# A shorter lag of the second matmuls, a later preparation in block 0, and a rearranged boot and end in a fused RWKV-6 and tanh-shrink kernel

## The chip, the cores and the metric

The kernel runs on one core of a Trainium2 chip. The metric is the device time of one execution in microseconds (us). Below, PE is TensorE, DVE is VectorE, ACT is ScalarE, POOL is GpSimd and SP is SyncE, as the profile has them.

## The reference

The first part is a recurrence over time steps in each of 4 batches and 8 heads, with a state of 48 x 48. The second part is a dense layer of 384 to 2048 to 384 over the 3072 tokens, with `h - tanh(h)` between its two matrix products.

```python
# r, k, v, w: (4, 8, 768, 48), u: (8, 48), all float32
for t in range(S):
    cur = np.einsum('bhd,bhe->bhde', u[None] * kt, vt)
    y[:, :, t] = np.einsum('bhd,bhde->bhe', rt, state + cur)
    state = wt[:, :, :, None] * state + np.einsum('bhd,bhe->bhde', kt, vt)
x = y.transpose(0, 2, 1, 3).reshape(3072, 384)
h = x @ w_in                    # (384, 2048)
out = (h - np.tanh(h)) @ w_out  # (2048, 384)
```

## The kernel before

The tokens are cut into 8 blocks of 384: two blocks (`q`) in each of four batches. A block's recurrence is computed in chunks of 64 tokens: masked products of keys and receptances inside a chunk (`own`, `earlier`), a state per chunk (`update_1` on PE, `update_2` on DVE), and results from states and from scores (`result`). The eight heads are four pairs, and the pairs are two halves, named 2 and 0 by their first pair. The block's preparation on DVE consists of running products of the decays: `behind` (line 300) with `inverse` (321, 323), `before` (289), and their products with keys and receptances, `times_behind` (314) and `times_before` (307). On ACT there are `times_u` (328) and `bound` (334).

The dense part of a block runs in 16 steps `f`. In a step, `first` (line 626) makes three matmuls with `w_in` into one PSUM tile `hp`, which ACT copies to `h`; `slight` (638) computes `s = h*h` with its largest value on DVE; `Second.add` (671) multiplies `g` with `w_out` into three accumulators. Every float32 matmul is two instructions in the profile. The operations after `s` (`qa` on ACT, `hs` and `gT` on DVE) are kept in `rest` and come behind the next step's `s`. The second matmuls of step f are put behind those of `first` of step f + LAG, through the list `waiting`; LAG is 4 before the change, also across the border of two blocks.

All queues (PE, DVE, ACT and SP) run in the order in which the program is written. While block i goes through its dense steps, block i + 1 (`later`) is prepared and its recurrence computed, at the steps that `plan` (685) lists: `before` names the preparations of a step, `phases` the parts that use PE, and `ahead` the first preparations for block i + 2 (`after`) in steps 13 and 14. `loads` names the load that is tied behind a step's `h`.

The first block has no such cover. `boot` (722) loads it, computes its recurrence and converts the first three of 16 pieces of the weights. A piece is converted (`convert`, 199) by three operations on ACT and two on DVE (a shift and an add). Pieces 3 to 15 are converted in block 0's steps 0 to 12, their two DVE operations one step later, through `extra`. The boot's PSUM tiles come from a pool of four buffers, which are handed out in turn; the dense part takes over this space when the boot is through.

At the end, DVE counts whether all of a set of bounds hold (`holds`, lines 839 to 842), PE sums the counts over the partitions (847), DVE makes a flag `again` of the sum (848), and every engine loads the flag (851), by which a second, general version of the whole computation is run or left out. It is left out here.

The tiles named `o`, from which a result's rows are stored (679 to 683), have three buffers.

## Time and profile before

| what | value |
|---|---|
| median of 4 runs | 614.78 us (613.43 to 615.81) |
| profiled execution, its own time | 614.5 us |
| its span | 612.7 us |
| PE busy | 586.4 us, 96% of the span |
| DVE busy | 378.3 us, 62% |
| ACT busy | 237.3 us, 39% |
| first dense matmul (line 629) | at 29.13 us |
| last second matmul (line 676) | ends at about 608 us |

A row of the profile's timeline gives the start, the duration, the engine, the line, the operation, the output and the inputs with their shapes, and in brackets the idle time of the engine ahead of it with what ended it. A row of the waits gives who waited for whom, the sum, the number of times and the longest. The slices on the page are fortieths of the span, 15.3 us each, and a digit is the busy share in tenths.

### The profile page before, as it was taken

Reading aid. Unit: us, or ns where it says so; the run is one execution under the profiler, and the core shown is the slowest. Engines: PE = TensorE matmul, PEld = TensorE weight load, DVE = VectorE, ACT = ScalarE, POOL = GpSimd, SP = SyncE. Lnnn points to the kernel's source line nnn. Section 1 sums busy time; section 2 is a strip of 40 time slices with the busy share of each in tenths; the row PEclk is TensorE's granted clock in tenths of the full one; section 3 lists DMA queues with packets and bytes.
Section 4 is the critical chain, followed back from the end, with each engine's and each line's share of the span. In section 5 each row is a group of like instructions: output and inputs, shape, how many; then the busy total and the mean of one; then the engine's idle time right before and its main releaser. Section 6 shows DMA issues by size and latency. Waiting matters only on the chain.

```text
span 612.7 us, 12671 instructions
## 1 busy us (share of the span) xinstructions
PE 586.4 (96%) x5410; PEld 363.0 (59%) x5410; DVE 378.3 (62%) x777; ACT 237.3 (39%) x444; POOL 11.4 (2%) x39
## 2 busy tenths in 40 slices
PE   3679899999999999999999999999999999999996
PEld 3536566566656665566655666566665666555553
DVE  8798996855377645766367563786447663444442
ACT  4879773333324323243323433252232532223222
POOL 6000000000000000000000000000000000000000
PEclk9879999999999999999999999999999999999999
DMA  8495542103202032111211122020321100001001
GB/s 316 148 358 179 174 152 68 57 22 105 64 0 79 2 106 61 40 40 49 67 53 39 41 73 96 0 78 2 105 62 36 43 2 5 8 0 39 1 0 42
DMA packets 23420, 43.03 MB, mean 70 GB/s; under 512 B 2112, under 2 KB 21312, under 8 KB 23360
## 3 DMA queue, kind: packets, MB, share of 16 engines
q1 hardware_dynamic: 22944, 41.89, 20.7%
q8 instruction: 43, 0.70, 0.5%
q10 hardware_dynamic: 352, 0.25, 0.1%
q14 instruction: 17, 0.14, 0.1%
q0 software_dynamic: 64, 0.05, 0.0%
HBM read 36.28 MB, written 4.72 MB: 67 GB/s over the span
## 4 chain that ended last, share of the span: by engine, by line
PE 89%; ACT 4%; DVE 3%; POOL 1%; issue 1%; PEld 1%; ACTq 0%; PEldq 0%; DVEq 0%; POOLq 0%
PE acc L676 39%; PE hp L629 39%; PE att L363 3%; PE att L469 2%; PE att L405 2%; PE att L486 2%; PE att L386 2%; POOL mask_all L144 1%; ACT up L208 1%; ACT w_sb L205 1%; ACT up L209 1%; ACT h L632 1%; DVE w_sb L213 0%; DVE gT L635 0%; ACT qa L645 0%
## 5 line engine op out<-in xcount | busy, mean ns | idle before, releaser
L629 PE MATMUL hp<-xT,w_sb 128*128 128x384 f32 x768 | 274.0, 494 | 5.6 <-ACT h L632 2.5
L676 PE MATMUL acc<-w_sb,gT 128*128 128x384 f32 x768 | 271.1, 490 | 0.8
L629 PEld LDWEIGHTS hp<-xT,w_sb 128*128 128x128 f32 x768 | 146.3, 192 | 110.3 <-ACT h L632 8.2
L676 PEld LDWEIGHTS acc<-w_sb,gT 128*128 128x128 f32 x768 | 143.0, 190 | 95.3 <-issue 1.7
L643 DVE CUSTOM_DVE_ANT_0 s<-h 128x384 f32<-128x384 f32 x128 | 71.2, 556 | 196.3 <-ACT h L632 196.1
L632 ACT ACTIVATE h<-hp 128x384 f32<-128x384 f32 x128 | 62.6, 489 | 323.3 <-PE hp L629 323.3
L635 DVE SCALAR_TENSOR_TENSOR gT<-qa,hs 128x384 f32<-128x384 f32 x128 | 71.5, 559 | 16.7 <-PE acc L676 0.5
L645 ACT ACTIVATE qa<-s,shift 128x384 f32<-128x384 f32 x128 | 77.6, 606 | 0.1
L635 DVE SCALAR_TENSOR_TENSOR hs<-h,s 128x384 f32<-128x384 f32 x128 | 70.8, 553 | 0.0
L370 DVE COPY_PREDICATED scores<-mask_all,att 128x768 f32<-128x768 uint8 x32 | 30.5, 1005 | 1.0 <-PE att L363 1.0
L300 DVE TENSOR_TENSOR_SCAN post<-w,seed 128x780 f32<-128x780 f32 x16 | 28.5, 1782 | 0.0
L289 DVE TENSOR_TENSOR_SCAN pre<-w,start 128x780 f32<-128x780 f32 x16 | 28.5, 1780 | 0.0
L386 PE MATMUL att<-ident,post 128*128 128x128 f32 x96 | 13.4, 292 | 10.1 <-DVE post L314 10.1
L328 ACT ACTIVATE k<-k,u_sb 128x384 f32<-128x384 f32 x32 | 17.7, 602 | 7.2 <-DVE post L314 7.2
L386 PEld LDWEIGHTS att<-ident,post 128*128 128x128 f32 x96 | 11.9, 151 | 12.4 <-DVE post L314 10.1
L208 ACT ACTIVATE up<-raw 128x768 f16<-128x768 f32 x16 | 17.0, 1062 | 0.0
L209 ACT ACTIVATE up<-raw 128x768 uint16<-128x768 uint32 x16 | 16.8, 1048 | 0.0
L213 DVE CUSTOM_DVE_ANT_0 w_sb<-w_sb,up 128x1536 uint16<-128x1536 uint16 (+1 forms) x17 | 15.5, 912 | 1.3 <-DVE w_sb L212 0.6
L405 PEld LDWEIGHTS att<-v_sb,ks 64*64 64x64 f32 x704 | 12.5, 139 | 6.0 <-issue 3.8
L519 ACT COPY late<-att 128x384 f32<-128x384 f32 (+1 forms) x9 | 4.3, 477 | 30.0 <-PE att L486 28.4
L363 PEld LDWEIGHTS att<-r,k 48*64 48x64 f32 x768 | 13.2, 145 | 4.5 <-issue 3.8
L428 DVE TENSOR_TENSOR states<-states,att 128x192 f32<-128x192 f32 x40 | 14.2, 354 | 2.2
(52 smaller groups left out, 262.3 us busy)
## 6 DMA issues: line engine op xcount, KB each, us to landing
raw<-in_weights SPq DMA_DIRECT2D x16, 768.0 KB, 5.2
w<-in_wT SPq DMA_DIRECT2D x7, 780.0 KB, 5.0
k<-in_kT SPq DMA_DIRECT2D x7, 768.0 KB, 4.4
r<-in_rT SPq DMA_DIRECT2D x7, 768.0 KB, 4.7
v_sb<-in_v SPq DMA_DIRECT2D x8, 576.0 KB, 3.8
out_y<-o SPq DMA_DIRECT2D x23, 192.0 KB, 2.0
xT<-late SPq DMA_DIRECT2D x44, 24.0 KB, 1.9
w<-in_wT SPq DMA_DIRECT2D x2, 390.0 KB, 4.9
```

The costliest lines, as they stand in the source:

```text
L289: return nc.vector.tensor_tensor_scan(out=self.tile("pre")[:, cols], data0=self.tile("w")[:, cols], data1=start[:, cols], initial=0.0, op0 ...
L300: return nc.vector.tensor_tensor_scan(out=back(t[:, 0:width]), data0=back(self.tile("w")[:, a:a + width]), data1=back(seed[:, a:a + width] ...
L363: nc.tensor.matmul(dst, lhsT=self.chunk(lhs, p, 2 * c + par)[rows], rhs=src, start=True, stop=True)
L370: return lambda: nc.vector.copy_predicated(out=A[:, :, p0:p0 + UP].rearrange("s h p c t -> s h (p c) t"), mask=mask.to_broadcast([P, 2, UP ...
L386: nc.tensor.transpose(tp[:, p, c * P:(c + 1) * P], self.chunk("post", p0 + p, 2 * c, n=2), ident)
L405: nc.tensor.matmul(kvp[64 * h:64 * h + 64, par, n0:n0 + D], lhsT=ks[toks, p % UP, c, 64 * h:64 * h + 64], rhs=self.v[toks, c, e0:e0 + D], ...
L629: nc.tensor.matmul(hp, lhsT=w_in_sb[:, f, kc, :], rhs=xT[kc], start=(kc == KC - 1), stop=(kc == 0))
L632: return h, nc.scalar.activation(out=h, in_=hp, func=AF.Copy, scale=1.0 / UPSCALE)
L635: return lambda: nc.vector.scalar_tensor_tensor(out=out, in0=in0, scalar=scalar, in1=in1, op0=op0, op1=ALU.mult)
L643: nc.vector.tensor_tensor_reduce(out=s, in0=h, in1=h, scale=1.0, scalar=0.0, op0=ALU.mult, op1=ALU.max, accum_out=top[:, n:n + 1])
L645: return g, [lambda: nc.scalar.activation(out=qa, in_=s, func=AF.Square, bias=shift[:, 4:5]), product(hs, h, TOP, s, ALU.mult), product(g, ...
L676: nc.tensor.matmul(acc, lhsT=g[:, j * P:(j + 1) * P], rhs=w_out_sb[:, f, :], start=(f == 0), stop=(f == NF - 1))
```

## The change

- `LAG` goes from 4 to 2, and with it the number of `gT` buffers from 5 to 3. The `h` tiles have three buffers instead of four.
- The boot no longer computes `behind` and `inverse` of block 1's half 2, and gives the two DVE operations of the third weight piece to `extra`, so that they come in step 0 behind its `s`.
- In block 0's plan, the two halves of `behind` and `inverse` come in steps 2 and 3, and what follows them moves by one to three steps; `update` now comes before `own`. The other blocks' plans stay.
- In the boot, `update_1` puts the first chunk pair in one PSUM tile and the other two in a second, where it was the first two and the third. `earlier` of half 0 comes behind the first part of the results from states; `later.bound(h2)` comes before them. The last four copies are divided by pair between DVE and ACT, where they were divided by rows.
- At the end, most of the flag's sum is made in the last block's step 14. The rest of it and its matmul stand before the remaining operations of the last step and ahead of both second matmuls that are left.
- The last 128 rows' copy is divided by columns between ACT and DVE, each with a tile `o` and a store of its own.

```diff
-LAG = 4
+LAG = 2
...
-        def update_1(self, ps):
+        def update_1(self, ps, parts=((0, 1), (2,))):
             last = self.q == NQ - 1
-            for cs in ((0, 1), (2,)):
-                kvp = self.kv[cs[0]] = scratch(ps)
+            for cs in parts:
+                kvp = scratch(ps)
+                for c in cs:
+                    self.kv[c] = kvp[:, :, (c - cs[0]) * NPAIR * D:(c - cs[0] + 1) * NPAIR * D]
...
-                    copy = engines[len(copies) % len(engines)] if engines else nc.scalar.copy
-                    copies.append(copy(out=dst[rows], in_=src[rows]))
+                    copies.append(engines[p % len(engines)](out=dst[rows], in_=src[rows]))
...
-        h = dense.tile([P, NB], F32, name="h", tag="h", bufs=4)
+        h = dense.tile([P, NB], F32, name="h", tag="h")
...
                 if f == NF - 1:
+                    rows = slice(self.row0 + j * P, self.row0 + j * P + P)
+                    if rows.stop == N:
+                        for at, engine in ((slice(0, DM // 2), nc.scalar), (slice(DM // 2, DM), nc.vector)):
+                            o = dense.tile([P, DM], F32, name="o", tag="o")[:, at]
+                            if engine is nc.scalar:
+                                nc.scalar.activation(out=o, in_=acc[:, at], func=AF.Copy, scale=1.0 / UPSCALE)
+                            else:
+                                nc.vector.tensor_single_scalar(o, acc[:, at], 1.0 / UPSCALE, op=ALU.mult)
+                            queue = nc.scalar if engine is nc.scalar else nc.sync
+                            queue.dma_start(out=out[rows, at], in_=o)
+                        continue
...
-            phases = {5: "turn", 8: "own", 9: "update", 11: "earlier", 13: "result 1"}
-            before = {0: ("behind 0", "inverse 0"), 1: ("times_behind 2",), 2: ("times_behind 0",),
-                      4: ("before 2",), 5: ("times_u 2",), 6: ("before 0", "times_u 0"),
-                      7: ("times_before", "held")}
+            phases = {6: "turn", 8: "update", 10: "own", 12: "earlier", 13: "result 1"}
+            before = {2: ("behind 2", "inverse 2"), 3: ("behind 0", "inverse 0"), 4: ("times_behind 2",),
+                      5: ("times_behind 0",), 6: ("before 2",), 8: ("times_u 2",), 9: ("before 0", "times_u 0"),
+                      10: ("times_before", "held")}
...
-        blk.update_1(ps)
+        blk.update_1(ps, ((0,), (1, 2)))
...
         later.bound(h1)
-        blk.result("from_states", ALL, cs=(0, 1), more=True)
+        later.bound(h2)
+        blk.result("from_states", ALL, cs=(0,), more=True)
         earlier = blk.earlier(ps, h2)
+        blk.result("from_states", ALL, cs=(1,), more=True)
         blk.result("from_states", ALL, cs=(2,))
         earlier()
         blk.result_out(both[0], True)
-        later.bound(h2)
...
-        ins = blk.result_out(both[1], True, [nc.scalar.copy, nc.vector.tensor_copy])
+        ins = blk.result_out(both[1], True, (nc.vector.tensor_copy, nc.scalar.copy))
...
-        later.prepare("behind 2")
-        later.prepare("inverse 2")
-        converted()
+        return ready.pop()
...
-    waiting, rest, extra = [], [], []
+    waiting, rest, extra = [], [], third
...
+            if not later and f == NF - 2:
+                at = n_whole + n_excess
+                nc.vector.tensor_single_scalar(holds[:, n_whole:at], excess, 0.0, op=ALU.is_le)
+                sum_held(holds[:, at:at + n_top - 2], top[:, 0:n_top - 2], holds[:, 0:at + n_top - 2], ends[:, 0:1])
...
+    sum_held(ends[:, 1:3], top[:, n_top - 2:], ends, count)
+    sure = ps_a.tile([P, 2, BANK], F32, name="att", tag="att")
+    again = const.tile([1, 1], I32, name="again", tag="again")
+    nc.tensor.matmul(sure[0:1, 0, 0:1], lhsT=count, rhs=ones, start=True, stop=True)
     for op in rest:
         op()
...
     for n, (s, fs, gs) in enumerate(waiting):
-        if n == 1:
-            nc.tensor.matmul(sure[0:1, 0, 0:1], lhsT=count, rhs=ones, start=True, stop=True)
...
         if n == len(waiting) - 1:
             anew = nc.values_load(again, min_val=0, max_val=1)
```

## The prediction

> **What bounds the kernel now.** I read the page's slices first, then a table of windows, the waits, and the timelines of the boot, of block 0 and of the end.

> ```profile
> PE   3679899999999999999999999999999999999996
> DVE  8798996855377645766367563786447663444442
> PEclk9879999999999999999999999999999999999999
> ```

> TensorE is full from the sixth slice on. Whatever changes must change in the first 100 us or in the last 15.

> ```profile
> 20.00:40.00 20.00, 14.64 (x243) 8.57 (x232) 15.31 (x32) 14.33 (x24) 1.24 (x4) 0.66 0.63 221
> 40.00:50.00 10.00, 7.17 (x22) 3.59 (x21) 9.69 (x18) 10.00 (x15) 0.00 (x0) 1.00 0.78 273
> 60.00:70.00 10.00, 9.90 (x122) 6.02 (x121) 9.66 (x17) 9.82 (x14) 0.00 (x0) 1.00 0.63 223
> 160.00:230.00 70.00, 69.89 (x663) 43.48 (x662) 43.94 (x91) 22.71 (x47) 0.13 (x2) 1.00 0.17 54
> ```

> Columns: window, length, then PE, PEld, DVE, ACT, POOL busy, granted clock, DMA share, GB/s. In block 1 (160 to 230) VectorE is busy for 44 of 70 us; in block 0 (40 to 70) it and ScalarE have no room at all, since they also convert the weights. The 0.66 is half speed from 25 to 38.5 us.

> ```profile
> PE hp L629 <- ACT h L632: 2.5, 3, 1.3
> PE att L405 <- DVE scores L370: 1.6, 1, 1.6
> PE hp L629 <- DVE w_sb L213: 1.5, 1, 1.5
> ```

> These are PE's named waits of block 0, 5.6 us; of the first line, twice 0.58 lie between the first three steps, where no second matmul exists yet. The rest is all that a shorter lag or another order could fill there.

> ```profile
> 28.04 1.03 DVE L519 COPY xT<-att 48x384 f32<-48x384 f32 x2 [2.04 <-ACT xT L519]
> 29.13 4.21 PE L629 MATMUL hp<-xT,w_sb 128*128 128x384 f32 x6 [1.53 <-DVE xT L519]
> 31.52 1.78 DVE L300 TENSOR_TENSOR_SCAN post<-w,seed 128x780 f32<-128x780 f32 x1
> 42.63 0.55 DVE L643 CUSTOM_DVE_ANT_0 s<-h 128x384 f32<-128x384 f32 x1
> 91.52 1.63 PE L469 MATMUL att<-pre,states 48*64 48x64 f32 x96
> ```

> The first dense matmul waits for the boot's last copy; the scan at 31.52 runs in time in which VectorE has nothing else to do; step 2 of VectorE begins at 42.63; the result phase of block 0 begins at 91.52.

> **Boot: -0.4 us.** PE stands from 21.46 to 22.85 for "issue", which the new order of the partial products seems to be aimed at. I give it nothing: the page's instruction queue moves 0.70 MB in 43 packets for 10,820 loads and matmuls, so about 65 B each and some 254 a packet, and between this pause and the one that ended at 19.11 lie 254 of them. That is code arriving, and the code is as long after the change (bounds: 0 to -1.4, taken 0, since the count fits). `bound(h2)` leaves ScalarE's queue at 26.48 (1.13 us), so ScalarE's copies of pair 1 are done by about 27.4. VectorE now takes both copies of pair 0, after PE's last score matmul (27.59), and no longer waits for ScalarE until 28.04: 27.65 + 1.03 = 28.68. The first dense matmul moves from 29.13 to 28.74.

> **Block 0: +1.1 us.** Per step VectorE spends 0.48 (`s`), 0.67 (`hs`), 0.48 (`gT`) from start to start, and 0.59 and 0.87 for a weight's conversion: 3.09. PE spends 2 x 1.94 = 3.87. A phase adds about 1.5 to PE. The preparation costs VectorE, from the rows: `behind` and `inverse` of a half 2.05, `times_behind` of a half 0.87, `before` of a half 1.70, `times_before` and `held` 1.75, own mask 1.85, update 11 x 0.39 = 4.3, earlier mask 1.8. Of this, before ran `behind` and `inverse` twice (4.1) by 38.4, beside PE's two half-speed steps (4.2 us each), where they cost nothing. The change leaves VectorE idle there: it is through with the boot's conversions at about 31.1, `s` of step 0 comes at 33.7, the third conversion (1.5) follows, `s` of step 1 at 38.6. That is 5.6 us idle, and the 4.1 us come back in steps 2 and 3.

> From step 2 it is a race. ScalarE sets its start: `h`, `qa` and a conversion take 3.5 us a step (42.05 to 45.55 in the timeline), so `s` of step 2 stands at about 42.1, 0.5 before the old 42.63. VectorE then has, through step 12, 11 x 3.09 = 34.0, plus 2 x 2.05 + 2 x 0.87 + 1.70 (steps 2 to 6), 4.3 (8), 1.70 (9), 1.75 + 1.85 (10), 1.8 (12) = 18.9: 52.9, ending at 95.0. In steps 7 and 8 it waits for `h` for about 1.3 (0.5 and 0.8 by following the queues step by step): 96.3, and the result phase, which needs the last mask, starts at about 96.5. PE alone would be there at 40.6 + 22 x 1.94 + 6.0 (four phases) = 89.2, so VectorE decides. What PE loses between its first dense matmul and the results is what its work leaves of that time: 91.52 - 29.13 - (8.4 + 21 x 1.94 + 6.0) = 7.2 before, 96.5 - 28.74 - (8.4 + 23 x 1.94 + 6.0) = 8.7 after. The old waits of 1.3, 1.5 and 1.6 are filled by the early second matmuls or fall with the new order, and new ones stand before the second matmuls of steps 2 and 3 (1.9), the turn (1.8), the own and earlier phases (0.3), the second matmul of step 12 (0.9) and the results (2.5). The old kernel was at this place at 91.52 with two second matmuls fewer behind it, so at 91.52 + 3.87 = 95.39 by the same work. 96.5 - 95.4 = +1.1, in which the boot's -0.4 is contained. Bounds: if VectorE never waits after 42.1, 95.2: -0.2; if each of the waits for `h` costs double, +2.4. After this PE leads again.

> The other moves have one answer. Update ahead of own takes away the 1.57 us that PE waited for own's masks at 72.5 (counted above). Loads keep their steps and their order on SP; `w` of block 2 (step 11) must wait for `before 0`, now step 9, still two steps ahead. POOL's memsets move with `behind` and are 0.1 us each.

> **Blocks 1 to 7: 0.** With lag 2, `gT` must be done one step and a phase after its `h`. In the last plain step PE finished `hp` at 597.31 and `gT` of the step before ended at 599.20 + 0.56 = 599.76, that is 2.45 later, where the slot comes 3.87 later: 1.4 us spare. The update (4.3 us on VectorE) takes the idle 2.1 and its phase's 1.55 first; the next `s` is then late by 0.1 (139.27 in block 1), so the spare stays. Three `gT` and three `h` buffers suffice: each is read at least a step before its reuse. If this cover were gone, 0.3 us in each of seven blocks would be 2 us.

> **The end: +1.3 us.**

> ```profile
> 599.20 0.56 DVE L635 SCALAR_TENSOR_TENSOR gT<-qa,hs 128x384 f32<-128x384 f32 x1
> 601.17 0.50 DVE L842 TENSOR_REDUCE count<-holds 128x1 f32<-128x336 f32 x1
> 601.93 6.07 PE L676 MATMUL acc<-w_sb,gT 128*128 128x384 f32 x18
> 608.04 0.49 ACT L681 ACTIVATE o<-acc 128x384 f32<-128x384 f32 x1 [0.15 <-PE acc L676]
> ```

> Count from the end T of the last `hp` (597.31). Before: two second matmuls, the flag's at +4.5, three more until +10.43; idle 0.5. After, one fits behind T (until +1.94); then PE stands at the flag's matmul, which now precedes the others in its queue: `gT` of step 14 is through at +2.37, the two small flag operations take about 0.4 (0.17 and less by the 16-column row), the matmul runs at +2.87. Two second matmuls follow from +2.98 and end at +6.86; the last `gT` (+3.9) and the flag's load (0.5, from +4.0) are in time. Two of the five have moved ahead of T (3.87): 6.86 + 3.87 - 10.43 = +0.3. The early sums (0.9 us on VectorE in step 14) lie in its 2.14 us of idle time: 0.

> The last row block's copy is split, so four `o` tiles are asked for in block 7, with three buffers. The fourth, VectorE's half, takes that of row block 0, whose store goes out at 607.27 and lands 2.0 later: 609.3. The copy (0.35, by a 128x192 row) and a store of 2.0 end at 611.7, where the old store was issued at 608.56 and landed 2.2 later at 610.76: +1.0. If the buffer were free, halves of 0.3 instead of 0.49 would give -0.2 instead: ends -0.2 and +1.2, taken +1.0, since the three buffers are in the code.

> **Sum.** 1.1 + 0.3 + 1.0 = +2.4, rounded to +2.5 with the flag's handshake. The profiled execution took 614.5 (span 612.7, 1.8 around it), 0.3 under the median of 614.78: **617.0 us**. What can be told from no change here is 0.3%, 1.84 us.

> [...] The granted clock is 0.50 from 26 to 38 us, with PE busy throughout 30 to 32 and 34 to 38; it is full only at 38.5, 9.4 us after the first dense matmul. So I keep 4.2 us for the first two steps. [...]

> **Rivals.**
> The clock stays full through the boot (0.10): step 2's `s` would come at 38.4, set by ScalarE's 3.5 a step, not at 42.1; block 0 would gain 2.6 to 3.0 where I add 1.1, giving 612.8 to 613.2. Against it: the pauses at 21.5 and 24.4, behind which the clock fell, stand.
> The lag pays (0.10), faster: the waits of 1.3, 1.53 and 1.57 vanish and VectorE keeps up, because its back-to-back operations overlap more than in the rows: -4.4 - 0.4 + 1.3 = -3.5, 611.0. It decides if VectorE needs under 47 us for steps 2 to 12. Against it: DVE 9.66 of 10 in 60 to 70.
> The fourth output buffer is free (0.16): 615.8, about no change.
> [...]
> Forecast (0.50): 615.5 to 618.5.

> **Numbers.** Faster by over 0.3%: the lag 0.10, half of the clock and a little of the forecast's low end, 0.17. Slower: 0.35 of the forecast, the late clock, a little else: 0.52. The rest 0.31. The range leaves out the paying lag and a little at the top: 612.5 to 619.6.

> **What would show it.** Right: DVE idle between 31 and 38, PE waits for `gT` (L635), `post` and the masks between 48 and 97, results at 96.5; blocks 1 to 7 at 69.9 of 70; PE waiting 0.9 for `count`; VectorE's last copy 1 us after ScalarE's. Wrong: PE without waits between 45 and 97, a granted clock of 1.00 at 29, or stalls on `gT` in later blocks.

## The result, and the profile after

The changed kernel takes 616.3 us (median of 52 runs, 613.65 to 619.77), the kernel before 614.03 us in the same comparison (median of 76, 613.07 to 616.55). The ratio is 1.0028, with a 95% interval of 1.0021 to 1.0035: slower by 1.7 us (1.3 to 2.15), surely more than nothing, and by the middle value just inside the 0.3% that the prediction called no change. The profiled execution after the change took 615.41 us (span 613.7), 0.9 us more than the one before.

The page's slices of the changed kernel:

```profile
PE   3697998999999999999999999999999999999995
DVE  8779897756368553766367563685537764444442
PEclk9899999999999999999999999999999999999999
```

The table of windows (window, length, PE, PEld, DVE, ACT, POOL busy, granted clock, DMA share, GB/s):

```profile
20.00:40.00 20.00, 14.20 (x242) 8.74 (x231) 13.17 (x28) 16.46 (x27) 1.24 (x4) 0.83 0.62 222
40.00:50.00 10.00, 9.51 (x31) 5.32 (x30) 9.62 (x16) 10.00 (x15) 0.00 (x0) 1.00 0.88 325
60.00:70.00 10.00, 10.00 (x108) 6.22 (x107) 8.34 (x16) 7.91 (x13) 0.00 (x0) 1.00 0.38 128
160.00:230.00 70.00, 69.89 (x610) 43.31 (x601) 43.93 (x91) 24.13 (x49) 0.13 (x2) 1.00 0.18 54
```

Block 1 (160 to 230) has the same 69.89 as before. The first row holds the boot and the first steps: VectorE has 2.1 us less to do there (15.31 before), which is the work that was put off, and the granted clock is 0.83 where it was 0.66. That last figure isn't owed to the change, since the clock differs from one execution to the next: the mean of a run goes from 0.984 to 0.997 in the changed kernel and from 0.985 to 0.995 in the one before. It most likely explains why this execution is only 0.9 us longer.

TensorE's named waits from 27 to 110 us, who waited for whom, sum, times, longest:

```profile
PE acc L677 <- DVE gT L636: 2.2, 3, 1.1
PE att L471 <- DVE scores L371: 1.9, 2, 1.3
PE att L387 <- DVE post L315: 1.5, 1, 1.5
PE hp L630 <- DVE xT L520: 1.5, 1, 1.5
PE hp L630 <- ACT h L633: 1.4, 2, 0.8
```

Before, two of the waits of block 0 named VectorE's masks and the conversion, and three ScalarE's `h`. Now three lines, 5.6 us, name VectorE's dense chain, its decays and its masks.

The timeline of the boot and of block 0:

```profile
27.59 1.12 DVE L520 COPY xT<-att 48x384 f32<-48x384 f32 x2 [1.98 <-ACT xT L520]
28.92 3.97 PE L630 MATMUL hp<-xT,w_sb 128*128 128x384 f32 x6 [1.47 <-DVE xT L520]
33.51 0.56 DVE L644 CUSTOM_DVE_ANT_0 s<-h 128x384 f32<-128x384 f32 x1 [2.26 <-ACT h L633]
36.52 0.56 DVE L644 CUSTOM_DVE_ANT_0 s<-h 128x384 f32<-128x384 f32 x1 [0.98 <-ACT h L633]
40.03 0.56 DVE L644 CUSTOM_DVE_ANT_0 s<-h 128x384 f32<-128x384 f32 x1 [0.35 <-ACT h L633]
43.12 1.78 DVE L301 TENSOR_TENSOR_SCAN post<-w,seed 128x780 f32<-128x780 f32 x1
46.97 2.20 PE L677 MATMUL acc<-w_sb,gT 128*128 128x384 f32 x6 [0.49 <-DVE gT L636]
52.19 2.20 PE L677 MATMUL acc<-w_sb,gT 128*128 128x384 f32 x6 [1.07 <-DVE gT L636]
58.49 0.88 PE L387 MATMUL att<-ident,post 128*128 128x128 f32 x6 [1.51 <-DVE post L315]
88.30 2.20 PE L677 MATMUL acc<-w_sb,gT 128*128 128x384 f32 x6 [0.65 <-DVE gT L636]
93.78 0.33 PE L471 MATMUL att<-pre,states 48*64 48x64 f32 x4 [1.35 <-DVE scores L371]
94.67 1.61 PE L471 MATMUL att<-pre,states 48*64 48x64 f32 x92 [0.56 <-DVE scores L371]
```

The `s` rows show VectorE waiting 2.26, 0.98 and 0.35 us for ScalarE's `h`, in the time in which the scan at 31.52 stood before. The scan comes at 43.12 instead. From there TensorE runs into VectorE at every place that the prediction named but the own and earlier phases, and the results begin at 93.78, with another 0.56 lost in their middle.

The end:

```profile
602.37 0.56 DVE L636 SCALAR_TENSOR_TENSOR gT<-qa,hs 128x384 f32<-128x384 f32 x1
603.04 0.16 DVE L812 TENSOR_REDUCE count<-ends 128x1 f32<-128x3 f32 x1
603.35 0.19 PE L859 MATMUL att<-ones,count 128*1 128x1 f32 x2 [0.82 <-DVE count L812]
603.46 4.14 PE L677 MATMUL acc<-w_sb,gT 128*128 128x384 f32 x12
607.64 0.33 ACT L685 ACTIVATE o<-acc 128x192 f32<-128x192 f32 x1 [0.15 <-PE acc L677]
608.82 0.36 DVE L687 TENSOR_SCALAR o<-acc 128x192 f32<-128x192 f32 x1 [4.41 <-DMA out_y<-o]
609.21 0.34 SPq L689 DMA_DIRECT2D out_y<-o  x1
```

VectorE's half of the last copy waits for a DMA, the store whose buffer it takes, and starts 1.18 us after ScalarE's half. From TensorE's end to the end of the span are 6.1 us (613.7 - 607.6); before, 4.7 (612.7 - 608.0).

### The profile page after: what moved, and what is told of

Same layout as the page of the kernel before. It is cut to its first block, busy times and chain, and to the rows that moved or that the text cites. A ratio compares the mean times of both kernels' runs of the same rounds, so it can differ in the third digit from the quotient of the medians.

```text
span 613.7 us, 12808 instructions
## 1 busy us (share of the span) xinstructions
PE 583.4 (95%) x5410; PEld 361.5 (59%) x5410; DVE 379.0 (62%) x780; ACT 238.4 (39%) x444; POOL 11.4 (2%) x39
## 4 chain that ended last, share of the span: by engine, by line
PE 83%; DVE 10%; issue 2%; ACT 2%; POOL 1%; DMA 0%; PEld 0%; ACTq 0%; DVEq 0%; PEldq 0%; POOLq 0%
PE acc L677 38%; PE hp L630 37%; PE att L364 3%; PE att L488 2%; PE att L408 2%; PE att L387 1%; DVE s L644 1%; DVE hs L636 1%; DVE w_sb L214 1%; POOL mask_all L144 1%; DVE scores L371 1%; DVE gT L636 1%; DVE post L301 1%; ACT h L633 1%; DVE w_sb L213 1%
## 5 line engine op out<-in xcount | busy, mean ns | idle before, releaser
L364 PEld LDWEIGHTS att<-pre,post 48*64 48x64 f32 x768 | 12.8, 140 | 5.5 <-issue 4.9
L471 PEld LDWEIGHTS att<-pre,states 48*64 48x64 f32 (+1 forms) x768 | 12.1, 133 | 6.2 <-issue 3.3
```

The lines of the kernel that those rows point to most:

```text
L364: nc.tensor.matmul(dst, lhsT=self.chunk(lhs, p, 2 * c + par)[rows], rhs=src, start=True, stop=True)
```

## The experiments

The theory under test is the prediction's: the plan's later preparation makes VectorE late in block 0 and costs more than the shorter lag brings, the divided store adds about 1 us, the boot and the flag give a little. Its rivals: that the lag itself costs or that the plan is harmless, and that the boot's new order takes away the pause of TensorE ahead of the last scores. A third theory, on the clock, came up after the second group. In each group the kernel before was run beside the others: 614.88, 614.07 and 614.05 us. Ratios are against it, with 95% intervals; differences of medians and of ratios can part by some tenths of a microsecond, and where they do, both are given.

### First group: lag, plan, buffers

**The kernel before, with the lag alone (e1_lag).**

```diff
-LAG = 4
+LAG = 2
```

> The old kernel with LAG = 2 alone. Theory 1 (a race of VectorE in block 0: the lag pays, the new plan costs): block 0 loses 3.7 us of PE's waits, since the old plan does 4.1 us of preparation beside the half-speed steps; the end gets 1.05 us longer, since the flag's whole sum (0.9 us) now stands behind the last gT and before the last second matmul. Sum -2.6 us, about 611.4 where the old kernel has 614.0. Theory 2 (the short lag itself is what costs: gT comes too late in any order, and the new plan is its remedy): 616 or more, with PE waits for gT in block 0.

Measured: 611.5 us, ratio 0.9951 (0.9934 to 0.9967). TensorE's waits from 28 to 110 us, besides 1.8 for the boot's last copy:

```profile
PE att L405 <- DVE scores L370: 1.6, 1, 1.6
PE hp L629 <- ACT h L632: 1.2, 2, 0.6
```

No wait for `gT`: under the old plan VectorE keeps up with a lag of two, and the early second matmuls fill the old waits of 1.3 and 1.5. That for own's masks (1.6) stays. The lag by itself is a gain of 3.0 us (2.1 to 4.1).

**The kernel before, with block 0's new plan alone, lag 4 (e2_plan).**

```diff
-            phases = {5: "turn", 8: "own", 9: "update", 11: "earlier", 13: "result 1"}
-            before = {0: ("behind 0", "inverse 0"), 1: ("times_behind 2",), 2: ("times_behind 0",),
...
+            phases = {6: "turn", 8: "update", 10: "own", 12: "earlier", 13: "result 1"}
+            before = {2: ("behind 2", "inverse 2"), 3: ("behind 0", "inverse 0"), 4: ("times_behind 2",),
...
-        later.prepare("behind 2")
-        later.prepare("inverse 2")
-        converted()
+        return ready.pop()
```

> The old kernel with block 0's new plan alone: behind and inverse in steps 2 and 3, the third conversion in step 0, update ahead of own; LAG stays 4. Theory 1: VectorE reaches the results at 96 to 97 us as in the changed kernel, but without two second matmuls done earlier: +5.0 us, about 619. Theory 2: with four steps of room nothing waits for VectorE, so within 1 us of 614.0.

Measured: 621.78 us, ratio 1.012 (1.0097 to 1.0144), the slowest kernel of the study, and 2 to 3 us beyond what the race of VectorE explains. Its table of windows shows the rest (granted clock in the third column from the right):

```profile
60.00:64.00 4.00, 4.00 (x13) 2.37 (x12) 3.83 (x7) 2.20 (x3) 0.00 (x0) 0.62 0.27 108
98.00:100.00 2.00, 1.92 (x77) 1.73 (x70) 1.86 (x4) 0.00 (x0) 0.00 (x0) 0.62 0.65 242
100.00:102.00 2.00, 2.00 (x4) 1.08 (x4) 2.00 (x2) 0.00 (x0) 0.00 (x0) 0.53 0.00 0
```

Twice within block 0, long after the start, the clock falls to half for one stretch of about 3.4 us with TensorE busy (from 60.9 to 64.3 and from 98.5 to 101.9, by the clock of the windows, which is 0.92 from 64 to 66 and 1.00 from 102 on): each costs some 1.7 us, an estimate (half of the stretch). This was foreseen by neither theory.

**The changed kernel with four `o` buffers (e3_four_o):** `bufs=4` for the tiles `o`.

> The changed kernel with four buffers for the o tiles. Theory 1: the last copy no longer waits for the store of row block 0 (1.2 us) and ends with ScalarE's half: 1.2 to 1.4 us less than the changed kernel, about 615.0. Rival: the wait is not on the path that sets the end (the end is then ScalarE's half or the closing semaphores): no change, 616.3.

Measured: 615.34 us, ratio 1.0016 (1.0000 to 1.0031), under the changed kernel by 1.0 in the medians and 0.7 in the ratios, whose intervals overlap. The timeline of its end:

```profile
608.61 0.33 ACT L685 ACTIVATE o<-acc 128x192 f32<-128x192 f32 x1 [0.15 <-PE acc L677]
608.97 0.36 DVE L687 TENSOR_SCALAR o<-acc 128x192 f32<-128x192 f32 x1 [3.59 <-ACT o L685]
609.37 0.34 SPq L689 DMA_DIRECT2D out_y<-o  x1
```

The wait for the DMA is gone, but the halves still don't run side by side: VectorE now waits for ScalarE, and starts after it is through. From TensorE's end (608.57) the span goes on for 5.2 us instead of 6.1, still not less than the 4.7 of the undivided copy. No run here has the two copies at the same time, so what an overlap would do isn't shown.

**The changed kernel with the old plan and the old boot preparation (e4_old_plan):** the edit of e2_plan, taken back.

> The changed kernel with block 0's old plan and the old preparation in the boot; lag 2, the boot's tiles and copies and the new end stay. Theory 1: -3.7 in block 0, -0.4 in the boot, +0.3 and +1.4 at the end: -2.4 against the old kernel, about 611.6, that is 4.7 under the changed kernel. Theory 2: at least as slow as the changed kernel, 616.3 or more, with PE waits for gT.

Measured: 611.94 us, ratio 0.9956 (0.9940 to 0.9973). The plan thus costs 4.4 us of the changed kernel (616.3 - 611.94), more than the whole difference.

### Second group: boot, beginning, flag

**The kernel before, with the boot's tiles, order and copies alone (e5_boot):**

```diff
-        blk.update_1(ps)
+        blk.update_1(ps, ((0,), (1, 2)))
...
-        blk.result("from_states", ALL, cs=(0, 1), more=True)
+        later.bound(h2)
+        blk.result("from_states", ALL, cs=(0,), more=True)
...
-        ins = blk.result_out(both[1], True, [nc.scalar.copy, nc.vector.tensor_copy])
+        ins = blk.result_out(both[1], True, (nc.vector.tensor_copy, nc.scalar.copy))
```

> The old kernel with the boot's new PSUM tiles, order of partial products, bound and last copies alone; LAG 4 and the old plan stay. Theory 1 (PE's pause of 1.4 us near 21.5 is code arriving, so the new order cannot close it; only the copies gain): the first dense matmul 0.2 to 0.4 us earlier, the sum -0.2 to -0.4 us. Theory 2 (the pause is a wait for the states and the earlier mask's matmuls fill it): the pause goes, first dense matmul near 27.5, -1.5 us.

Measured: 613.11 us, ratio 0.9985 (0.9974 to 0.9995), -0.9 us (-1.6 to -0.3). Its timeline:

```profile
22.34 0.69 PE L363 MATMUL att<-pre,post 48*64 48x64 f32 x32 [0.97 <-issue]
28.33 4.18 PE L629 MATMUL hp<-xT,w_sb 128*128 128x384 f32 x6 [1.46 <-DVE xT L519]
```

The pause for "issue" stays, at about the same time, so the new order does not remove it. What the order does can be read from the twelve profiles: from the end of this pause to the first dense matmul it is 6.28 or 6.29 us in the four with the old boot, and 5.69 to 6.03 (mean 5.87) in the eight with the new one, -0.4. The pause itself lasts 0.55 to 1.39 us in the old kind and 0.87 to 1.52 in the new, and ends at 22.5 (old) and 22.4 (new) on average. The interval of the runs takes in the predicted -0.4; its middle is about double, and the rest isn't accounted for.

**The changed kernel, `behind` and `inverse` begun in steps 0 and 1 (e6_begin0):**

```diff
-            before = {2: ("behind 2", "inverse 2"), 3: ("behind 0", "inverse 0"), 4: ("times_behind 2",),
+            before = {0: ("behind 2", "inverse 2"), 1: ("behind 0", "inverse 0"), 4: ("times_behind 2",),
```

> The changed kernel with behind and inverse of the two halves in steps 0 and 1 in place of 2 and 3; everything else stays, also update ahead of own and the crowd of steps 9 to 12. Theory 1: VectorE works where it now stands idle; by following the queues, 2.4 of the 4.9 us come back that the plan costs: 613.9 where the changed kernel has 616.3. PE's waits for gT in steps 2 and 3 and for the turn shrink from 3.7 to about 1.3, the 2.3 to 2.5 us before the results stay. Rival (VectorE's whole sum decides, not its place): the results start as late as before, 616.3.

Measured: 616.14 us, ratio 1.0034 (1.0022 to 1.0046): a miss of 2.2 us. Yet the timeline shows the expected gain up to the results, and then a loss:

```profile
91.27 0.33 PE L471 MATMUL att<-pre,states 48*64 48x64 f32 x4 [1.35 <-DVE scores L371]
92.16 2.78 PE L471 MATMUL att<-pre,states 48*64 48x64 f32 x92 [0.56 <-DVE scores L371]
95.03 4.19 PE L677 MATMUL acc<-w_sb,gT 128*128 128x384 f32 x6
```

The results begin 2.5 us earlier than in the changed kernel's profile (91.27 against 93.78), of which about 1 is the earlier first dense matmul of this execution (27.96 against 28.92), but then take 2.78 us instead of 1.61, and the next second matmul 4.19 instead of 2.20. The windows say why:

```profile
88.00:92.00 4.00, 2.25 (x10) 0.97 (x9) 3.83 (x7) 0.99 (x2) 0.00 (x0) 1.00 0.13 12
92.00:94.00 2.00, 1.84 (x70) 1.84 (x74) 1.90 (x6) 0.00 (x0) 0.00 (x0) 0.56 0.91 316
94.00:96.00 2.00, 1.91 (x35) 1.42 (x30) 1.97 (x3) 0.00 (x0) 0.00 (x0) 0.50 0.19 64
96.00:98.00 2.00, 2.00 (x5) 1.09 (x4) 1.24 (x3) 0.00 (x0) 0.00 (x0) 0.50 0.00 0
```

TensorE had been busy for 2.25 of the 4 us ahead, in waits of 1.35 and 0.56 us, and the clock went to half for 6.8 us (92.3 to 99.1). From this came the third theory: the crowded waits ahead of the results let the clock fall, and this, not VectorE's lateness alone, is what a plan for block 0 can lose.

**The kernel before, with lag 2 and the early sum of the flag (e7_flag):** the last three parts of the change's diff on top of e1_lag, with the last copy undivided.

> The old kernel with LAG = 2 and the flag's early sum, and nothing else. The flag's matmul then stands ahead of both remaining second matmuls. Theory 1: with the short lag the early sum pays: PE's work ends 6.9 us behind the last hp matmul where LAG = 2 alone has 7.5, -0.65 us against it, 610.9. Rival: PE's new wait of 0.8 us for the count eats it, 611.5.

Measured: 610.7 us, ratio 0.9950 (0.9937 to 0.9963). By the median that is 0.8 less than e1_lag, by the ratio 0.1 less, both within what two groups can differ by, so the profile has to decide: from the start of the last `hp` to TensorE's end it shows 9.7 us in e1_lag (595.69 to 605.40) and 9.1 in this kernel (594.87 to 603.94). In e1_lag a matmul stands for 0.77 us waiting for `again`; here the matmul of the flag waits 0.77 for `count`, but there is no second stall behind it. The first line is e1_lag's, the others are this kernel's:

```profile
603.23 2.17 PE L676 MATMUL acc<-w_sb,gT 128*128 128x384 f32 x6 [0.77 <-DVE again L848]
599.68 0.19 PE L851 MATMUL att<-ones,count 128*1 128x1 f32 x2 [0.77 <-DVE count L804]
599.80 4.14 PE L677 MATMUL acc<-w_sb,gT 128*128 128x384 f32 x12
```

By these two profiles the flag's move is worth 0.6.

**The parts that pay, together (e8_best):** lag 2, the old plan, the new boot, the early flag, one undivided last copy.

> Lag 2, block 0's old plan, the boot's new tiles and copies, the early flag, and the last rows' copy undivided on ScalarE as before. With four o buffers VectorE's half still began only when ScalarE's half had ended, so the division gains nothing. Theory 1: the last store goes out 1.4 us earlier behind PE's end than with the divided copy and three buffers: 1.4 to 1.7 us under the 611.9 of the same kernel with the division, 610.3; the fastest of all. Rival (the end is set by the closing semaphores): 611.9.

Measured: 610.48 us, ratio 0.9943 (0.9930 to 0.9957), the lowest median of the study (e7_flag's 610.7 can't be told from it): 3.5 us (2.6 to 4.3) under the kernel before. Against e4_old_plan, which differs only in the divided copy, that is 0.8 us by the ratios and 1.5 by the medians, and the intervals overlap. The span after TensorE's end is 5.1 us (608.7 - 603.6), again about one less than with the divided copy.

### Third group: the clock

Both kernels get three matmuls more in block 0, whose results nobody reads: one behind the earlier masks' phase of step 12, two ahead of the results of step 13. They fill the stretch in which TensorE waits for masks; the rest of the program stays.

```diff
+    def hold(xT, n):
+        hp = ps_d.tile([P, NB], F32, name="hp", tag="hp")
+        for _ in range(n):
+            nc.tensor.matmul(hp, lhsT=ident, rhs=xT[0], start=True, stop=True)
...
+                if i == 0 and f == 13:
+                    hold(here, 2)
                 if f in phases:
                     later.phase(ps_a, phases[f])
+                if i == 0 and f == 12:
+                    hold(here, 1)
```

**On e6_begin0 (e9_hold0).**

> The kernel with behind and inverse in steps 0 and 1 (616.14), and in block 0 three more matmuls (identity by a block of x into the free hp tile, 0.65 us each, their result is not used) where PE waits in any case: one behind the earlier masks of step 12, two ahead of the results in step 13. Theory 3 (PE's waits at 85 to 92 us let the granted clock fall to half for 6.8 us, which costs 3.4 and hides what the earlier preparation gains): the clock stays full there and 2 to 3.4 us come back, 613 to 614. Rival (the order of VectorE alone decides): the extra work changes nothing or adds up to 0.6 us, 616.1 to 616.7.

Measured: 613.62 us, ratio 0.9992 (0.9981 to 1.0004), 2.5 us less than e6_begin0. The windows of this kernel, around its results at 92.39:

```profile
92.00:94.00 2.00, 2.00 (x98) 1.61 (x96) 1.90 (x6) 0.00 (x0) 0.00 (x0) 1.00 0.87 251
94.00:96.00 2.00, 1.91 (x14) 1.06 (x6) 1.97 (x4) 0.00 (x0) 0.00 (x0) 1.00 0.39 143
96.00:98.00 2.00, 2.00 (x99) 1.57 (x98) 1.61 (x3) 0.35 (x1) 0.00 (x0) 1.00 0.00 0
```

More work in the same place made the kernel faster, and the clock stays at 1.00. This shows the clock's fall to be the cause in e6_begin0.

**On the changed kernel (e10_hold).**

> The changed kernel with the same three extra matmuls. Theory 3: its runs spread from 613.65 to 619.77 because the clock falls near 92 us in a part of them; with the extra matmuls the runs over 617 go, and the median comes to about 615.2. The profiled execution, in which the clock did not fall there, would hardly change. Rival: the spread comes from the boot's clock alone: median 616.3 or up to 0.6 more, and runs over 617 as before.

Measured: 616.35 us, ratio 1.0026 (1.0010 to 1.0041): the median doesn't move (616.3). What changes is the top: the changed kernel has 12 of 52 runs above 617.01, this one none of 12 (613.65 to 617.01). By chance alone that would happen some 4 times in 100 (40/52 to the twelfth), or oftener, since the limit was set after the runs. So the falling clock may make the longest runs of the changed kernel, which isn't shown, and it does not make its median. Its results stand at 95.53, in one piece behind the extra matmuls:

```profile
95.53 1.74 PE L471 MATMUL att<-pre,states 48*64 48x64 f32 x96
```

With the clock held in both, beginning in steps 0 and 1 instead of 2 and 3 is worth 2.7 us by the medians (616.35 - 613.62) and 2.1 by the ratios. That leaves some 1.7 to 2.3 of the plan's 4.4, which the crowd of preparations in steps 9 to 12 may cost, since both kernels have it. That remainder was not tried by itself.

## Why the prediction was right

**Block 0, +1.1.** Right in its mechanism: the sum has both that the early second matmuls fill the old waits and that VectorE, late by the new plan, makes new ones. The runs split the two. The lag does pay (e1_lag, -3.0), and the plan takes more than that back (4.4). The rival "the lag pays" was true of the lag and failed only at its condition, that VectorE keeps up: under the new plan it does not. The single waits, predicted and in the profile: `gT` of steps 2 and 3 1.9 and 1.56 (0.49 + 1.07), the turn 1.8 and 1.51, the second matmul of step 12 0.9 and 0.65, the results 2.5 and 1.91 (1.35 + 0.56), own and earlier 0.3 and none. Each is a little high, and the size of the term is the least certain part. e1_lag's -3.0 contains an end that is longer by 0.95 (from the end of the last `hp`, 597.63, to TensorE's end, 605.40, are 7.77; before, 597.31 to 608.00 less 3.87 for two more second matmuls are 6.82), so in block 0 the lag gains about 3.9, an estimate. With the plan's 4.4 and the boot's -0.4 that leaves +0.1 where +1.1 was put; the two sums are known to about 1 us each, so that the runs don't decide between the two figures. The results were put at 96.5 and stand at 93.78 in this profile, because step 2's `s` comes at 40.03 and not at 42.1: the granted clock was full from 32.6 us on, not from 38.5. In the profile of e3_four_o, where it is full from 36.6 on, the results stand at 94.75. By this the profile should be faster than the median, and it is (615.41 against 616.3). What the two profiles differ by agrees: at the results, the changed one is at 94.3 with the middle pause, where the old one by the same work is at 95.4 (-1.1), and the end gives back 1.4 and 0.3; +0.6 against +0.9 measured.

**The clock through the boot.** Held as half speed until 38.5 for the sum. The chances also count a full clock through the boot and a late one, and no run shows the late one: in the ten profiles whose windows or rows show where the half-speed stretch ends, that is between 30.8 and 32.9 us in five and between 36.6 and 38.5 in the other five, with old and new boots on both sides. It is a draw for each execution. In the changed kernel the runs go with it: of 54, 20 runs with a mean clock of 0.994 lie between 614.2 and 615.7, the 11 with 0.991 between 616.0 and 616.9, the 10 with 0.986 and 0.987 between 616.9 and 619.8. The kernel before spreads over 3.5 us in all, the changed one over 6.1, and a straight line through the runs gives 0.38 us for each 0.001 of mean clock in the changed kernel and 0.17 in the one before (the 60 runs of it in the three groups). The likely reason is that with the scan gone from the first steps, VectorE has nothing to do there but wait for `h`, and so the whole block begins when the clock allows it; e9_hold0, which has the scan there, with 0.29 against e10_hold's 0.33 does not settle it. This spread is in no term of the sum.

**The boot, -0.4.** The pause was given nothing, and rightly: it is still there, with 1.52 us.

```profile
22.89 0.70 PE L364 MATMUL att<-pre,post 48*64 48x64 f32 x32 [1.52 <-issue]
```

In the traces of the two kernels it comes behind TensorE's 697th load or matmul before the change (348 matmuls and 349 loads by 21.4 us) and behind the 696th after it (348 and 348), though different work stands there. That fits code arriving in blocks, and not a wait for a tile; what arrives was not tested. VectorE's last copy starts at 27.59, just behind TensorE's last score matmul (27.46), as forecast; the ScalarE copy that its row names had ended at 26.50. The first dense matmul was put at 28.74 and stands at 28.92; by the twelve profiles the order and the copies are worth the 0.4, by e5_boot's runs 0.9 (0.3 to 1.6).

**Blocks 1 to 7, 0.** Right: 69.89 of 70 in block 1, and behind 110 us TensorE's only named wait is the one for `count`.

**The end, +0.3, and the store, +1.0.** From the end of the last first matmul, here 600.43, the flag's matmul starts at +2.92 (predicted +2.87), after a wait of 0.82 (0.9), and TensorE's next two second matmuls end at 607.60, +7.2 by the row and +6.9 if each takes its slot of 1.94 (predicted +6.86). The store costs 1.4 in the profile (6.1 against 4.7); the runs, 0.7 to 1.0 for the buffer (e3_four_o) and 0.8 to 1.5 for the division (e8_best against e4_old_plan), agree without fixing it. Two terms were mis-sized: the halved store lands in 2.6 us on SP's queue where 2.0 was assumed, and the bound of -0.2 with a free buffer was wrong in sign, since the halves of one accumulator were copied one after the other (e3_four_o: 608.97 after 608.94, and 5.2 us against 4.7).

**The sum.** +2.5 was predicted against the profiled execution; the medians give +2.3 and the ratio +1.7. That this is slower is right; that it is so by more than 0.3% is not settled, since the interval has that bound in it. That 617.0 lies so near 616.3 is partly luck: by the estimate above block 0 may have been put about 1 too high, the store was up to 0.4 too low, and single executions lie up to 6.1 us apart, mostly with the clock, for which one value was taken.

**What was not in it:** that the clock can fall again within block 0, as it did behind crowded waits of TensorE in e2_plan (at 98.5 us, behind 1.75 and 0.56) and e6_begin0 (at 92.25, behind 1.35 and 0.56). The falls cost e2_plan's profiled execution about 3 us, an estimate, and e6_begin0 2.5 by e9_hold0, and such a fall may account for the changed kernel's longest runs, which isn't shown.

## What to carry to other kernels

A shorter lag and a later preparation draw on the same spare time of the engine that feeds TensorE: cost them together, but try them apart, since here one gains 3.0 us and the other loses 4.4. Work that runs beside a stage that waits for something else is free only there; moved behind it, it comes back as waits. Before dividing a last copy, look at the buffer that each part takes and whether the parts run side by side (in e3_four_o VectorE's began at 608.97 us, when ScalarE's had ended at 608.94), and where many short waits stand close together, look at the granted clock behind them (0.50 for 6.8 us in e6_begin0).
